# Splitting the last two heads' output product into two token halves, one for each column group of TensorE

## The chip, the cores and the metric

The kernel runs on one core of one Trainium2 chip. The metric is the device time of one execution in microseconds (us). Executions of the kernel before agree within 0.6%. For a comparison of ratios, runs of the kernel before and of the other kernel were taken in the same rounds on the same chip.

The engines are named as in the profile: PE is TensorE (matmuls), PEld its weight loads, DVE is VectorE, ACT is ScalarE, POOL is GpSimd.

## The reference

For 2048 tokens of width 640 the reference mixes two branches with a per-token gate. Branch A is linear attention with 32 heads of width 20 and softmax feature maps; branch B is a SwiGLU feed-forward network (FFN). What matters here is the end of branch A:

```python
phi_q = jnp.concatenate([_softmax(pq, axis=-1), _softmax(-pq, axis=-1)], axis=-1)
kv = jnp.einsum("bhsf,bhsd->bhfd", phi_k, v)
z  = jnp.einsum("bhsf->bhf", phi_k)
num = jnp.einsum("bhqf,bhfd->bhqd", phi_q, kv)      # the output product
den = jnp.einsum("bhqf,bhf->bhq", phi_q, z)[..., None] + 1e-6
o = num / den
# ... o @ wo is branch A; g * a + (1 - g) * b
```

## The kernel before

Tokens come in four query tiles (`bt`) of 512. For each, `oitem` computes the output product in three parts. Three heads have 3 x 40 = 120 features, so a group of three heads takes one 120-row matmul with 60 useful outputs (64 columns). Ten groups cover 30 heads; group 10 holds the last two heads, with 80 rows and 40 columns.

```python
def oitem(bt, part):
    buf = bt % 2
    pr = next_pair()                 # a pair of PSUM banks, least recently used of four
    pairs = []
    ms = [2 * part, 2 * part + 1]
    for i, m in enumerate(ms):
        for s in range(2):
            j = 2 * m + s
            if j >= NCH:             # NCH = 11
                continue
            if j == NCH - 1:         # the last two heads
                l, o = kvsb[0:80, j, 0:40], bank(2 * pr + i, 0, 512, 64, 104)
                r = phiT[0:80, buf, :, j, :]
            else:                    # output at partition 0 or 64: column group 0 or 64
                l, o = kvsb[0:120, j, :], bank(2 * pr + i, 0, 512, 64 * s, 64 * s + 64)
                r = phiT[0:120, buf, :, j, :]
            pairs.append((o, l, r, True, True, False))
    mm(pairs)
    if part < 2:
        copy("act", oT[:, buf, 2 * part:2 * part + 2, :], halves(pr, 512))
    else:
        copy("act", oT[:, buf, 4, :], bank(2 * pr, 0, 512))
        copy("act", hT[64:104, buf, 13, :], bank(2 * pr + 1, 0, 512, 64, 104))
```

The last two heads go into spare partitions of `hT`, the FFN's hidden tile, so that one contraction of the down-projection covers both. That projection (`ditem`, 128 tokens each) reads `hT` and `oT`, and issues all its matmuls in one call, so TensorE waits for all its operands before the first of them:

```python
def ditem(bt, u):
    ...
    ls = [(hT[:, buf, k, tok], wd[:, k, :]) for k in range(13)]
    ls += [(hT[0:104, buf, 13, tok], wd[0:104, 13, :])]
    ls += [(oT[:, buf, m, tok], wog[:, m, :]) for m in range(5)]
    ...
    mm([p for ab in zip(*half) for p in ab])
```

Waits come from a small tracker. For PSUM it works by whole banks, and a reader also waits for another engine's earlier readers of the same bank:

```python
if space == "psum":
    lo = lo // BANK * BANK
    hi = (hi + BANK - 1) // BANK * BANK
...
for k in rkeys:
    for kk in self._conflicts(k):
        req(self.lastw[kk], True)
        if k[0] == "psum":
            for s, v in self.readers[kk].items():
                req((s, v), False)
```

The order of issue is one long list, in which every engine takes its work in the order written. Around the first block (`C4` is the softmax normaliser of token tile 4 on VectorE, `O0.x` the three parts of the output product, `B5` and `A6` the next VectorE feature work, `D0.1` the first down-projection tile):

```
... Q6 F0.11 C4 O0.0 O0.2
c4 B5 A6 O0.1 C5 c5 Q7 Q8 B6 C6 c6 D0.1 B7 Q9 D0.3 ...
```

The softmax here doesn't subtract the row's maximum and nothing guards it: scores larger than these inputs give would overflow.

## Time and profile before

| | before |
|---|---|
| median of the first 3 runs (of 6) | 288.79 us (288.93 us) |
| span of the profiled run | 287.3 us |
| TensorE busy | 284.5 us (99%) |
| an output block, first matmul to the next stage | 1.42 us |
| first block to the first down-projection tile | 4.15 us |

The chain of work that ended last, in order of time, shows how complete the bound is. The columns are start, duration and what ran:

```profile
77.41 0.05 PE ps L308
77.46 207.92 PE ps L296 x1271
285.38 0.03 issue
285.41 0.32 DVE osb L733
```

From 77.46 us on there is a single piece of 208 us of TensorE work without a gap.

### The profile page before, as it was taken

The numbers are of one execution on the slowest core, as the hardware profiler recorded it, in microseconds if no ns is written. First come the engines' busy times: TensorE is split into PE (matmuls) and PEld (weight loads), VectorE is DVE, ScalarE is ACT, GpSimd is POOL, SyncE is SP. The second block draws the span as 40 slices with busy tenths as digits, with TensorE's granted clock in tenths as the row PEclk, the third lists the DMA queues.
The fourth block names the chain that finished last, engine by engine and source line by source line (L and its number), as shares of the span: only waits on it lengthen the run. The fifth ranks groups of instructions, "written<-read, shape, count | busy, mean of one in ns | idle before, by whom it ended". The sixth has DMA issues, their size and how long they took to land.

```text
span 287.3 us, 4960 instructions
## 1 busy us (share of the span) xinstructions
PE 284.5 (99%) x1975; PEld 174.7 (61%) x1975; DVE 163.4 (57%) x243; ACT 151.9 (53%) x252; POOL 159.9 (56%) x125
## 2 busy tenths in 40 slices
PE   8999999999999999999999999999999999999997
PEld 7667777675644545557775556675554446656776
DVE  2337748576569978589991565970317899000000
ACT  0767778576775566682535653225586552234112
POOL 8286999879446789836542438350754558501000
PEclk9999999999999999999999999999999999999999
DMA  7975797000010598202573002061020006210101
GB/s 236 200 117 120 114 292 257 3 1 2 2 47 0 130 283 162 50 2 50 68 155 73 3 1 50 2 155 37 2 50 0 3 1 123 52 46 0 49 23 48
DMA packets 48944, 21.62 MB, mean 75 GB/s; under 512 B 39384, under 2 KB 48792, under 8 KB 48920
## 3 DMA queue, kind: packets, MB, share of 16 engines
q1 hardware_dynamic: 47400, 20.43, 31.2%
q10 hardware_dynamic: 1520, 0.87, 1.0%
q8 instruction: 16, 0.26, 0.4%
q14 instruction: 8, 0.07, 0.1%
HBM read 9.29 MB, written 2.62 MB: 41 GB/s over the span
## 4 chain that ended last, share of the span: by engine, by line
PE 99%; DVE 0%; issue 0%
PE ps L296 97%; PE ps L478 1%; PE ps L308 1%; DVE osb L733 0%
## 5 line engine op out<-in xcount | busy, mean ns | idle before, releaser
L324 POOL TENSOR_TENSOR hT<-hT,us 128x512 bf16<-128x512 bf16 (+1 forms) x56 | 65.1, 1175 | 65.3 <-DVE hT L328 47.0
L328 DVE SCALAR_TENSOR_TENSOR hT<-hT,ps 128x512 bf16<-128x512 bf16 (+1 forms) x56 | 37.4, 682 | 67.0 <-ACT hT L314 53.3
L296 PE MATMUL ps<-xT,wg 128*128 128x512 bf16 x260 | 64.6, 379 | 0.0
L296 PE MATMUL ps<-xT,wu 128*128 128x512 bf16 x260 | 64.6, 379 | 0.0
L296 PE MATMUL ps<-wd,hT 128*128 128x320 bf16 (+2 forms) x462 | 63.9, 295 | 0.0
L324 POOL TENSOR_TENSOR ph<-eq,qc 128x1320 bf16<-128x1320 bf16 x16 | 42.4, 2648 | 25.6 <-DVE qc L638 20.8
L296 PEld LDWEIGHTS ps<-wd,hT 128*128 128x128 bf16 x462 | 44.5, 98 | 17.4
L296 PE MATMUL ps<-wqk,xT 128*128 128x320 bf16 x320 | 47.7, 299 | 0.0
L314 ACT ACTIVATE hT<-ps 128x512 bf16<-128x512 f32 (+2 forms) x60 | 35.7, 596 | 16.7 <-PE ps L296 16.5
L296 PEld LDWEIGHTS ps<-xT,wu 128*128 128x128 bf16 x260 | 25.4, 98 | 30.7
L314 ACT ACTIVATE us<-ps 128x512 bf16<-128x512 f32 (+1 forms) x56 | 33.5, 598 | 19.2 <-PE ps L296 18.2
L314 ACT ACTIVATE osb<-ps,omg 128x640 bf16<-128x640 f32 (+2 forms) x17 | 12.9, 758 | 55.7 <-PE ps L296 55.7
L296 PEld LDWEIGHTS ps<-xT,wg 128*128 128x128 bf16 x260 | 25.0, 98 | 27.8 <-ACT oT L314 0.8
L324 POOL TENSOR_TENSOR ekr<-ekr,krec 128x1280 bf16<-128x1280 bf16 x16 | 37.4, 2358 | 5.8 <-DVE krec L338 5.8
L296 PEld LDWEIGHTS ps<-wqk,xT 128*128 128x128 bf16 x320 | 30.5, 98 | 13.1 <-issue 0.4
L314 ACT ACTIVATE eq<-ps 128x640 bf16<-128x640 f32 x32 | 22.4, 704 | 20.8 <-POOL ph L324 10.7
L335 DVE TENSOR_REDUCE ksum<-ekr 128x64 f32<-128x1280 bf16 x16 | 23.5, 1470 | 11.7 <-ACT ekr L314 11.7
L314 ACT ACTIVATE ekr<-ps 128x640 bf16<-128x640 f32 x32 | 22.3, 704 | 8.7 <-PE ps L296 8.2
L335 DVE TENSOR_REDUCE qz<-eq 128x64 f32<-128x1280 bf16 x16 | 23.7, 1478 | 2.6 <-ACT eq L314 2.6
L296 PE MATMUL ps<-wog,oT 128*128 128x320 bf16 (+2 forms) x165 | 24.7, 294 | 0.0
L296 PE MATMUL ps<-wvg,xT 128*128 128x320 bf16 (+1 forms) x160 | 24.1, 299 | 0.0
L335 DVE TENSOR_REDUCE qw<-ez 128x64 f32<-128x1280 bf16 x16 | 23.6, 1476 | 0.0
(73 smaller groups left out, 189.4 us busy)
## 6 DMA issues: line engine op xcount, KB each, us to landing
out_dram<-osb SPq DMA_DIRECT2D x15, 160.0 KB, 1.9
wd<-in_B_w_down_dram SPq DMA_DIRECT2D x1, 2080.0 KB, 9.6
wg<-in_B_w_gate_dram SPq DMA_DIRECT2D x1, 1040.0 KB, 10.6
wu<-in_B_w_up_dram SPq DMA_DIRECT2D x1, 1040.0 KB, 12.8
wg<-in_B_w_gate_dram SPq DMA_DIRECT2D x1, 800.0 KB, 5.8
wu<-in_B_w_up_dram SPq DMA_DIRECT2D x1, 800.0 KB, 8.3
wog<-in_A_wo_dram SPq DMA_DIRECT2D x2, 375.0 KB, 7.1
xs<-in_A_x_dram ACTq DMA_DIRECT2D x3, 160.0 KB, 3.6
```

The source lines that it names most:

```text
L296: last = pe.matmul(o, lhsT=l, rhs=r, start=st, stop=sp_, skip_group_check=sk)
L308: last = pe.transpose(o, i, ident[0:k, 0:k])
L314: return run("act", lambda: act.activation(o, i, func, scale=scale), rd, [o])
L324: return run(e, lambda: eo.tensor_tensor(o, a, b, op), [a, b], [o])
L328: return run("dve", lambda: dve.scalar_tensor_tensor(out=o, in0=a, scalar=s, in1=b, op0=op0, op1=op1), rd, [o])
L335: return run("dve", lambda: dve.tensor_reduce(o, i, AX.X, ALU.add), [i], [o])
L478: last = pe.matmul(bank(2 * pr, 0, P), lhsT=c, rhs=c, start=True, stop=True)
```

## The change

An odd number of equal matmuls can't fill two column groups. The change cuts the odd one (the last two heads) into two halves of 256 tokens, one for each group. Since the halves then land in different partitions of the bank, it also cuts the copy out of PSUM in two, one on VectorE and one on ScalarE. The whole diff:

```diff
                 if j == NCH - 1:
-                    l, o = kvsb[0:80, j, 0:40], bank(2 * pr + i, 0, 512, 64, 104)
-                    r = phiT[0:80, buf, :, j, :]
+                    for g, p0 in enumerate((0, 64)):
+                        pairs.append((bank(2 * pr + i, 256 * g, 256 * g + 256, p0, p0 + 40),
+                                      kvsb[0:80, j, 0:40], phiT[0:80, buf, 2 * g:2 * g + 2, j, :],
+                                      True, True, False))
+                    continue
@@
             copy("act", oT[:, buf, 4, :], bank(2 * pr, 0, 512))
-            copy("act", hT[64:104, buf, 13, :], bank(2 * pr + 1, 0, 512, 64, 104))
+            copy("dve", hT[64:104, buf, 13, 0:256], bank(2 * pr + 1, 0, 256, 0, 40))
+            copy("act", hT[64:104, buf, 13, 256:512], bank(2 * pr + 1, 256, 512, 64, 104))
```

## The prediction

> **What bounds the kernel now.** I read the page first (busy shares, then the chain that ended last), then the timeline of each of the four places where the changed code runs, then the groups by form for durations.
>
> ```profile
> PE 284.5 (99%) x1975; PEld 174.7 (61%) x1975; DVE 163.4 (57%) x243; ACT 151.9 (53%) x252; POOL 159.9 (56%) x125
> PE 99%; DVE 0%; issue 0%
> ```
>
> The first line is the busy time of each engine, the second the shares of the chain that ended last. The whole span is one unbroken run of TensorE (PE) work. From 77 us to the end no matmul starts later than its pace allows, apart from the edges of the four output-product blocks below. So TensorE time taken out shortens the run one for one, and any new stall of TensorE lengthens it one for one.
>
> The changed product runs in four short blocks, one per query tile (called O0 to O3 here), of eleven matmuls each. The timeline of TensorE at two FFN groups and at O0:
>
> ```profile
> 220.72 1.24 PE L296 MATMUL ps<-xT,wg 128*128 128x512 bf16 x5
> 221.80 1.24 PE L296 MATMUL ps<-xT,wu 128*128 128x512 bf16 x5
> ...
> 126.00 1.49 PE L296 MATMUL ps<-phiT,kvsb 120*64 120x512 bf16 x11
> 127.11 0.38 PE L296 MATMUL ps<-phiT,kvsb 120*64 120x512 bf16 x1
> 127.42 0.31 PE L296 MATMUL ps<-wqk,xT 128*128 128x320 bf16 x1
> ```
>
> Five 512-wide matmuls of full width advance the clock by 221.80 - 220.72 = 1.08 us, 0.216 each. Eleven in O0 take 126.00 to 127.42 = 1.42 us, not 2.38: they run two at a time in the two column groups (outputs at partitions 0 and 64). Single records confirm it: starts come in pairs 3 to 11 ns apart, the pairs 0.216 apart. Group 0 has five of the eleven, group 64 has six, because the odd one (the last two heads, 80*40) also writes at partition 64. The last matmul, at 127.11, therefore runs alone: half the array idles for one 0.216 us slot in each block. That is what the change is after.
>
> Who empties the banks, at O0 (the timeline of ScalarE and VectorE, and TensorE's next stage):
>
> ```profile
> 127.42 2.75 PE L296 MATMUL ps<-wqk,xT 128*128 128x320 bf16 x19
> 128.20 0.59 ACT L314 ACTIVATE hT<-ps 40x512 bf16<-40x512 f32 x1
> 128.81 1.02 ACT L314 ACTIVATE oT<-ps 128x1024 bf16<-128x1024 f32 x1
> 129.15 0.28 DVE L638 SCALAR_TENSOR_TENSOR qc<-qz,g,qd 128x64 f32<-128x64 f32 x1
> 129.35 0.82 DVE L324 TENSOR_TENSOR ez<-eq,zb 128x1280 bf16<-128x1280 bf16 x1
> 130.15 2.74 PE L296 MATMUL ps<-wd,hT 128*128 128x320 bf16 x19
> ```
>
> The `wd,hT` row at 130.15 is the first down-projection tile after O0. Its code waits for every operand before its first matmul, and the last of them is the `oT` copy that ScalarE ends at 128.813 + 1.024 = 129.84. The margin is 0.31 us. Meanwhile VectorE is busy without a break with the normalisers of the softmax features until the `qc` row ends at 129.435.
>
> **What the Trainium skill says.** TensorEngine Tiling (Array Packing), section Key Properties: tiles work independently, and a change of tiling mode drains TensorE. The trace agrees with both: the pairs start within 11 ns, and a change of mode costs 0.096 us at each edge of a block (0.31 against 0.216). The same page, PSUM Bottleneck, says that tiling does not speed the emptying of PSUM and advises to use both ScalarE and VectorE; the change does that, and the trace shows where it will pinch. PSUM — Partial Sum Buffer, on bank collisions, says that two engines must not touch one bank in one 32-partition quadrant at once, while different quadrants are allowed. The new copies read partitions 0-39 and 64-103, different quadrants, but the kernel's bookkeeping guards by whole bank, reads against reads of another engine included. So the ScalarE copy must wait for the VectorE copy. VectorE: DVE Perf Modes, section Two Vector instructions with no wait between them: an instruction whose output starts in another quadrant than the last one's starts only when the earlier ones have finished. The new copy writes at partition 64 behind `qc` at partition 0, so I give it no overlap; no row of the kernel before shows this case.
>
> **The change part by part.**
>
> TensorE. One 80*40 matmul over 512 tokens becomes two of 256, one in each column group. Each group then has five full slots and a half: 5.5 x 0.216 instead of 6 x 0.216, so 0.108 us less per block, 0.43 us for four. The added weight load (99 ns for 40 columns in the trace) goes ahead beside other work, as the 109 ns loads of this block do now; it barely fits beside a 107 ns stream, so 0.108 is the most.
>
> ScalarE. The 40x512 copy (592 ns) becomes 40x256. From the 512- and 1024-wide rows (590 and 1022 ns) the slope is 0.84 ns per element, so about 592 - 256 x 0.84 = 377 ns. It saves 0.21 us on an engine that is not the bound.
>
> VectorE. A new copy of 40x256 from PSUM, f32 to bf16. The rows of that kind are 120x160 in 314 ns and 128x640 in 824 ns (the groups by form), 1.06 ns per element between them: 314 + 96 x 1.06 = 416 ns. Four of them are 1.7 us, and where they stand matters.
>
> The new wait, block by block. In program order the VectorE copy comes after all VectorE work issued before the block, and ScalarE stands still until it is done.
>
> At O0 the normaliser of tile 4 (1.48 us reduction and six small steps, ending with `qc` at 129.435) is issued just before the block. So: copy starts 129.435 + 0.035 (the usual gap between dependent VectorE steps) = 129.47 and ends 129.89; ScalarE follows 0.035 later (seen from VectorE to ScalarE), 129.92, + 0.377 = 130.30; the remaining `oT` copy starts 0.024 later and ends 130.32 + 1.024 = 131.35; TensorE follows about 0.07 later (median of ScalarE to weight load), 131.42. Before it was 130.146: **+1.27 us**, already net, since the 0.108 gained in this block only makes TensorE arrive earlier at the same wait.
>
> At O1, O2 and O3 VectorE has long been idle:
>
> ```profile
> 158.11 0.69 DVE L328 SCALAR_TENSOR_TENSOR hT<-hT,ps 128x512 bf16<-128x512 bf16 x1 [6.48 <-ACT hT L314]
> 201.96 0.68 DVE L328 SCALAR_TENSOR_TENSOR hT<-hT,ps 64x512 bf16<-64x512 bf16 x1 [9.51 <-ACT us L314]
> 260.23 0.69 DVE L328 SCALAR_TENSOR_TENSOR hT<-hT,ps 128x512 bf16<-128x512 bf16 x1 [14.48 <-ACT hT L314]
> ```
>
> Brackets give the idle time of VectorE before each row. Those gaps span the blocks at 153.6, 196.9 and 255.7. In O2 the matmul ends near 197.4, the copy near 197.85, and ScalarE, which first has an output scaling and an `oT` copy to do, comes to its half only at 198.28: no wait. O1 and O3 have the same order. But VectorE work that now runs ahead of the block must wait behind the copy: at O1 a 1.48 us reduction (to about 156.1, next VectorE row 158.1), at O2 a normaliser of 2.9 us (to about 200.8, next row 201.96). Both fit. So each gives its 0.108 us: **-0.32 us**.
>
> Sum: 1.27 - 0.32 = +0.95 us on 288.79, **289.7 us**.
>
> **The rivals.**
>
> Clean gain: no stall at O0, -0.43, 288.36 us. For it speaks that TensorE is the whole chain and that the other three blocks have room; against it the 0.31 us margin and the 1.75 us (128.17 to 129.92) for which ScalarE would have to stand. It would need the copy to find VectorE free. One in ten.
>
> Halves that don't run side by side, or whose weight loads show: 0 in place of -0.32, giving 290.1 us. For it speaks that 99 ns of loading hardly hides behind 107 ns; against it, that the groups already run separate queues and that loads of both groups overlap now. Two in ten, in part.
>
> Later knock-on: VectorE is dense until 151.6 and everything in it moves 0.45 us later; a feature tile or a PSUM pair could come late to TensorE. Against it: of the next stages the tightest pair is freed near 139.4, and TensorE wants it at 141.8 before the shift of 1.27. It would add some tenths, 290.0 to 290.4 us. One in ten.
>
> **Range and chances.** The centre is 289.7. The size of the stall is a sum of four read-off durations, each good to some tens of ns; the gains are at most 0.32. The three runs of before spread from 288.74 to 289.39, which is the larger part of the doubt. I take 288.9 to 290.2 for 8 in 10; the clean gain lies outside it. Two per cent would be 5.8 us, far beyond anything found: faster 0.005, same 0.985, slower 0.01.
>
> **What would show it.** Right: at O0 a VectorE copy of 40x256 into `hT` starting near 129.47, ScalarE's 40x256 copy behind it with an idle bracket of about 1.7 us put down to VectorE, the next `oT` copy near 130.3, and the down-projection tile starting near 131.4 after an idle stretch of TensorE of 1.2 to 1.4 us. In O1 to O3 the block shrinks from 1.42 to about 1.32 us, with no idle bracket on ScalarE's half copy. Wrong: the copy found in front of the normaliser, a TensorE gap elsewhere, or blocks that stay 1.42 us long.

## The result and the profile after

The changed kernel takes 290.09 us (289.69 to 290.15, 6 runs) against 288.93 us (288.72 to 289.39, 6 runs): the ratio is 1.0034, with a 95% interval of 1.0021 to 1.0047. A ratio is the mean time of one kernel's runs over that of the other's of the same rounds, so it is not quite the ratio of the medians quoted. By the 2% at which this study calls a kernel faster or slower it is "same"; but the interval lies wholly above 1, so it is a loss of about 1 us, clear of the noise.

The page of the changed kernel, busy shares and the chain's shares by engine:

```profile
PE 284.3 (99%) x1979; PEld 174.6 (61%) x1979; DVE 166.2 (58%) x247; ACT 151.0 (52%) x252; POOL 159.4 (55%) x125
PE 99%; issue 0%; DVE 0%
```

TensorE has four matmuls more and is busy 0.2 us less, yet the span went from 287.3 to 288.4 us. The busy shares hide the reason. The chain of the changed kernel in order of time shows it:

```profile
77.67 52.74 PE ps L296 x272
130.40 1.24 issue
131.65 154.91 PE ps L296 x1003
```

The one piece of 208 us is now two, with 1.24 us between them in which TensorE did nothing ("issue" means that the profile saw no single wait to name). What stands there is in the timeline of the changed kernel, TensorE first and then VectorE, ScalarE and GpSimd; a bracket gives the idle time before a row and what ended it:

```profile
126.20 1.39 PE L296 MATMUL ps<-phiT,kvsb 120*64 120x512 bf16 x12
127.51 2.89 PE L296 MATMUL ps<-wqk,xT 128*128 128x320 bf16 x20
131.65 3.97 PE L296 MATMUL ps<-wd,hT 128*128 128x320 bf16 x28 [1.24 <-issue]
...
129.35 0.28 DVE L638 SCALAR_TENSOR_TENSOR qc<-qz,g,qd 128x64 f32<-128x64 f32 x1
129.67 0.42 DVE L320 CAST hT<-ps 40x256 bf16<-40x256 f32 x1
130.12 2.70 DVE L324 TENSOR_TENSOR ez<-eq,zb 128x1280 bf16<-128x1280 bf16 x1
...
130.12 0.38 ACT L314 ACTIVATE hT<-ps 40x256 bf16<-40x256 f32 x1 [1.75 <-DVE hT L320]
130.52 1.02 ACT L314 ACTIVATE oT<-ps 128x1024 bf16<-128x1024 f32 x1
...
129.72 2.42 POOL L324 TENSOR_TENSOR ph<-eq,qc 128x1320 bf16<-128x1320 bf16 x1 [1.52 <-DVE qc L638]
```

Follow the chain backwards. The down-projection tile at 131.65 follows ScalarE's `oT` copy, which ends at 131.55. That copy stands behind ScalarE's half copy, which waited 1.75 us for VectorE's half copy. And that one stands behind the normaliser, whose last step is the `qc` row. The matmuls themselves did what was intended: the block takes from 126.20 to 127.51, 1.32 us in place of 1.42.

In the second block (same timeline, VectorE and ScalarE) the same copies cost nothing, because VectorE was idle and waited for TensorE, and ScalarE got to its half later and shows no bracket:

```profile
155.67 0.42 DVE L320 CAST hT<-ps 40x256 bf16<-40x256 f32 x1 [2.79 <-PE ps L296]
156.53 0.38 ACT L314 ACTIVATE hT<-ps 40x256 bf16<-40x256 f32 x1
```

**A sharper measure than the time.** The start-up varies from run to run: in the traces used here the first block's first matmul starts anywhere from 125.80 to 126.76 us. From that matmul on the traces repeat closely: the time from the first down-projection tile to the end differs by at most 0.012 us between kernels that have the same later blocks. So I compare two stretches in each trace: from the first block's first matmul to the first down-projection tile (called the *lead*), and from that tile to the end of the span (the *rest*). Start times are from the single records.

| kernel | lead, us | rest, us | lead + rest against before |
|---|---|---|---|
| before | 4.150 | 157.121 | |
| changed | 5.450 | 156.799 | +0.98 |

The lead lost 1.30 us and the rest gained 0.32 us.

### The profile page after: what moved, and what is told of

Its sections match the earlier page's. It is cut to its first block, busy times and chain, and to the rows that moved or that the text cites. A ratio compares the mean times of both kernels' runs of the same rounds, so it can differ in the third digit from the quotient of the medians.

```text
span 288.4 us, 4971 instructions
## 1 busy us (share of the span) xinstructions
PE 284.3 (99%) x1979; PEld 174.6 (61%) x1979; DVE 166.2 (58%) x247; ACT 151.0 (52%) x252; POOL 159.4 (55%) x125
## 4 chain that ended last, share of the span: by engine, by line
PE 99%; issue 0%; DVE 0%
PE ps L296 97%; PE ps L478 1%; PE ps L308 1%; DVE osb L737 0%
## 5 line engine op out<-in xcount | busy, mean ns | idle before, releaser
L324 POOL TENSOR_TENSOR ph<-eq,qc 128x1320 bf16<-128x1320 bf16 x16 | 41.8, 2615 | 28.5 <-DVE qc L638 23.8
L314 ACT ACTIVATE hT<-ps 128x512 bf16<-128x512 f32 (+2 forms) x60 | 34.9, 582 | 18.4 <-PE ps L296 16.4
```

The lines of the kernel that those rows point to most:

```text
L314: return run("act", lambda: act.activation(o, i, func, scale=scale), rd, [o])
L324: return run(e, lambda: eo.tensor_tensor(o, a, b, op), [a, b], [o])
```

## The experiments

The theory: all the loss is ScalarE waiting for the VectorE copy in the first block, because the copy stands behind the normaliser in VectorE's order; the split matmuls gain 0.108 us in each block. Rival A: the halves or their weight loads cost TensorE time. Rival B: the late VectorE work after the first block holds TensorE; it has something to it at first sight, as the feature product `ez` behind the copy took 2.70 us in place of 0.82. Eight kernels ran, all with right results, with five rounds each.

### Both copies on ScalarE

```diff
-            copy("dve", hT[64:104, buf, 13, 0:256], bank(2 * pr + 1, 0, 256, 0, 40))
+            copy("act", hT[64:104, buf, 13, 0:256], bank(2 * pr + 1, 0, 256, 0, 40))
```

> Matmul halves kept, both copies of the halves on ScalarE. My theory (all of the loss is ScalarE standing behind the VectorE copy at O0; the halves themselves gain 0.108 us per block): two copies of 0.38 take the place of one of 0.59, so the next oT copy ends 0.19 later than in the kernel before, and the first down-projection tile starts about 4.10 us after O0's first matmul (before 4.15, after 5.45); from O0's first matmul to the end about 0.37 us less than before, 288.5 us. Rival A (the halves or their added weight load cost TensorE time): at best as slow as before. Rival B (the VectorE stretch after O0 runs late and holds TensorE): also about as before or better, since nothing was added to VectorE; B does not separate here.

Measured: lead 4.127, rest 156.798, together -0.35 us. The timed median was 288.62 us against 289.03 (ratio 0.9988, interval 0.9971 to 1.0004, so not proven by the times alone). ScalarE's timeline shows its three copies one after the other, with no wait:

```profile
128.96 0.78 ACT L314 ACTIVATE hT<-ps 40x256 bf16<-40x256 f32 x2
129.76 1.02 ACT L314 ACTIVATE oT<-ps 128x1024 bf16<-128x1024 f32 x1
```

The lead is 0.03 us longer than expected and otherwise as the theory has it. Rival A falls: with the same halves and the same loads, the kernel is not slower.

### The copies alone

```diff
-            copy("act", hT[64:104, buf, 13, :], bank(2 * pr + 1, 0, 512, 64, 104))
+            copy("dve", hT[64:104, buf, 13, 0:256], bank(2 * pr + 1, 0, 256, 64, 104))
+            copy("act", hT[64:104, buf, 13, 256:512], bank(2 * pr + 1, 256, 512, 64, 104))
```

This is against the kernel before; the matmul stays whole.

> The matmul left whole, only the copy split (VectorE first half, ScalarE second half). My theory: the stall at O0 as in the changed kernel and no gain elsewhere: the down-projection tile 5.4 us after O0's first matmul, +1.25 us to the end, 290.2 us. Rival A (the halves cost): as fast as before, 288.9.

Measured: lead 5.467, rest 157.109, together +1.31 us; 290.08 us (ratio 1.0039, interval 1.0026 to 1.0052). The loss comes with the copies and without the halves. The timeline of ScalarE in this kernel has the same wait:

```profile
130.70 0.38 ACT L314 ACTIVATE hT<-ps 40x256 bf16<-40x256 f32 x1 [1.76 <-DVE hT L320]
```

### The two copies swapped

```diff
-            copy("dve", hT[64:104, buf, 13, 0:256], bank(2 * pr + 1, 0, 256, 0, 40))
             copy("act", hT[64:104, buf, 13, 256:512], bank(2 * pr + 1, 256, 512, 64, 104))
+            copy("dve", hT[64:104, buf, 13, 0:256], bank(2 * pr + 1, 0, 256, 0, 40))
```

> The whole change, with its two copy lines swapped: ScalarE copies its half first, VectorE second. The VectorE copy keeps its place behind the normaliser and stays just as late. My theory: ScalarE no longer waits for VectorE; the oT copy ends near its old time, the VectorE copy ends about 0.1 us before TensorE needs it; no stall, 0.108 gained in all four blocks, 0.43 us less than before: 288.5 us, 4.04 us from O0's first matmul to the down-projection tile. Rival B (the late VectorE stretch is what costs; the feature product after the copy took 2.70 us in place of 0.82): the copy still pushes that product behind GpSimd's, so the loss of some 1 us stays, 289.9 us.

Measured: lead 4.253, rest 156.797, together -0.22 us; 288.33 us against 289.03 (ratio 0.9981, interval 0.9969 to 0.9993). Its ScalarE and VectorE timelines:

```profile
128.19 0.38 ACT L314 ACTIVATE hT<-ps 40x256 bf16<-40x256 f32 x1
128.59 1.02 ACT L314 ACTIVATE oT<-ps 128x1024 bf16<-128x1024 f32 x1
...
129.46 0.42 DVE L320 CAST hT<-ps 40x256 bf16<-40x256 f32 x1
129.91 2.70 DVE L324 TENSOR_TENSOR ez<-eq,zb 128x1280 bf16<-128x1280 bf16 x1
```

Swapping two lines takes the stall away, although VectorE does the same work in the same order: the copy is as late as before and `ez` still takes 2.70 us. So rival B falls. The gain is 0.21 us short of the expectation, all of it in the lead. The VectorE copy ends at 129.88 and the down-projection tile starts at 130.24, not at the 130.03 that the expected lead of 4.04 us gives. The records of TensorE's own sequencer show why (they stand in the packed trace; no view prints them): three wait instructions start there at 129.918, 130.029 and 130.135, one after the other. The first is the wait for VectorE. The two after it had nothing left to wait for, since what they wait for had last been signalled at 129.63 or before, and still they cost 0.11 us each.

### The first block issued before the normaliser

```diff
-... Q6 F0.11 C4 O0.0 O0.2
+... Q6 F0.11 O0.0 O0.2 C4
 c4 B5 A6 O0.1 ...
```

> The whole change, with the two block parts of O0 issued before the normaliser of tile 4 instead of behind it, so that the VectorE copy stands before the normaliser. My theory: copy starts as soon as TensorE is done with the halves (some 1.0 us after O0's first matmul), no wait on ScalarE, 4.04 us to the down-projection tile, 0.43 us less than before: 288.5 us. The normaliser comes 0.8 us later, and the feature product behind it should again start before GpSimd and take 0.82 us. Rival A: no better than before. If normaliser lateness matters, TensorE stalls later on.

Measured: lead 4.044, rest 156.792, together -0.43 us; 288.43 us against 289.03 (ratio 0.9982, interval 0.9970 to 0.9994). This is the full gain of the halves. The copy now waits for TensorE, not the other way round, and the normaliser follows it:

```profile
127.26 0.42 DVE L320 CAST hT<-ps 40x256 bf16<-40x256 f32 x1 [0.39 <-PE ps L296]
127.70 1.49 DVE L335 TENSOR_REDUCE qw<-ez 128x64 f32<-128x1280 bf16 x1
...
130.56 0.82 DVE L324 TENSOR_TENSOR ez<-eq,zb 128x1280 bf16<-128x1280 bf16 x1
...
128.47 0.38 ACT L314 ACTIVATE hT<-ps 40x256 bf16<-40x256 f32 x1
```

`ez` is back at 0.82 us, and the later normaliser disturbs nothing. This kernel beats both the kernel before and the changed one, in the times as in the traces.

### The change in the first block alone, and in the last three alone

```diff
-                if j == NCH - 1:
+                if j == NCH - 1 and bt == 0:       # the other run: bt > 0
                     for g, p0 in enumerate((0, 64)):
...                                                 # else as before, in matmuls and copies
```

> The change in the first query tile's block alone, the other three as before. My theory: +1.3 us, 290.2 us; the down-projection tile 5.45 us after O0's first matmul; the other blocks 1.42 us long. If the loss were spread over the four blocks: about +0.25.

> The change in the last three blocks, the first as before. My theory: 0.32 us less than before, 288.6 us; 4.15 us from O0's first matmul to the down-projection tile, the other three blocks 1.32 us long, no new stall. If the loss were spread over the four blocks: about +0.75.

Measured for the first block alone: lead 5.454, rest 157.117, together +1.30 us; 289.92 us against 289.00 (ratio 1.0038, interval 1.0017 to 1.0060). For the last three alone: lead 4.150, rest 156.792, together -0.33 us; 288.46 us against 289.00 (ratio 0.9984, interval 0.9961 to 1.0007, so not proven by the times). The two add up to +0.97 us; the whole change has +0.98. The loss sits in the first block and nowhere else, and each of the others gives 0.33 / 3 = 0.11 us.

### The part with the last two heads last of the three

```diff
-... C4 O0.0 O0.2
-c4 B5 A6 O0.1 C5 ...
+... C4 O0.0 O0.1
+c4 B5 A6 O0.2 C5 ...
```

> The whole change, with O0's part that holds the last two heads issued after the other two parts. ScalarE then waits for VectorE with nothing behind it but its own half. My theory: the half copy still ends about 4.3 us after O0's first matmul because VectorE is as late as before, and the down-projection tile reads it: it starts about 4.37 after O0's first matmul, 0.22 later than before; with the gain of the other blocks -0.1 us in all, 288.8 us. If only the number of waits mattered and not what stands behind them, it would be as slow as the changed kernel.

Measured: lead 6.390, rest 156.793, together +1.91 us; 292.22 us against 289.00 (ratio 1.0098). I had missed that this edit also puts the copy behind `B5` and `A6`, the next feature product and reduction of VectorE, so the expectation didn't fit the kernel. The timelines of VectorE, ScalarE and TensorE:

```profile
131.80 0.42 DVE L320 CAST hT<-ps 40x256 bf16<-40x256 f32 x1
132.26 0.38 ACT L314 ACTIVATE hT<-ps 40x256 bf16<-40x256 f32 x1 [2.97 <-DVE hT L320]
132.59 0.70 PE L296 MATMUL ps<-wd,hT 128*128 128x320 bf16 x4 [2.19 <-DVE hT L320]
```

The copy moved from 3.47 us after the block's start (129.668 - 126.197 in the changed kernel) to 5.61 (131.803 - 126.195), and the lead grew from 5.45 to 6.39. It is a stronger form of the same fault: what counts is the copy's place in VectorE's order. Here the tile waits for VectorE's copy itself. Four of the six timed runs had a lower TensorE clock (told in the last section); the two at full clock, 290.71 and 290.92 us, are 1.7 and 1.9 us above the kernel before, in accord with the trace.

The next run does what that one was meant to do:

```diff
-... C4 O0.0 O0.2
-c4 B5 A6 O0.1 C5 ...
+... C4 O0.0 O0.1
+O0.2 c4 B5 A6 C5 ...
```

> The run before this moved the part with the last two heads too far: it also came behind the next feature product and reduction of VectorE, so the copy stood 2.1 us later in VectorE's order. Here that part comes last of O0's three, but still right behind the normaliser, so the VectorE copy is where the changed kernel has it. My theory: the copy runs about 3.47 to 3.89 us after O0's first matmul as in the changed kernel, ScalarE's half ends at about 4.30, and the down-projection tile starts at about 4.4 (4.37 plus up to 0.1 of TensorE's own waits), against 5.45 in the changed kernel; to the end about 161.2 us, 288.9 us timed. If what stands behind ScalarE's wait made no difference: 5.45.

Measured: lead 4.256, rest 156.792, together -0.22 us; 288.76 us against 288.93 (ratio 0.9991, interval 0.9978 to 1.0005, so not proven by the times alone). The wait of ScalarE is still there:

```profile
129.72 0.38 ACT L314 ACTIVATE hT<-ps 40x256 bf16<-40x256 f32 x1 [0.83 <-DVE hT L320]
```

Nothing that TensorE soon needs stands behind it any more, and 1.19 of the 1.30 us that the lead had lost are back. The lead is 0.14 us shorter than I expected, and for a reason that I had wrong: the first down-projection tile takes tokens 128 to 255, which lie in VectorE's half, so it does not read ScalarE's half at all. Indeed it starts at 130.055, before ScalarE's half copy ends at 130.103. It waits for VectorE's copy, which ends at 129.692; from there to the tile it is 0.363 us, as in the run with swapped copies (129.879 to 130.242, also 0.363).

### Not tried

The tracker could guard PSUM by quadrants of partitions in place of whole banks, which should take away ScalarE's wait with the copies left in their order. That was not built, so that it does, and what it gives, is not shown. Nor was a kernel tried that puts the two halves into different banks.

## Why the prediction was right

The time predicted was 289.7 us, in a range of 288.9 to 290.2; measured were 290.09 us. The forecast difference of +0.95 us measured +0.98 in the traces; the medians differ by 1.16. The time lies 0.4 us above the centre and only 0.11 below the range's upper end, so that it lay inside the range owes something to chance. What is known of the 0.4 us is not the mechanism: 0.14 is the kernel before, whose median was 288.79 in the first three runs and 288.93 in all six, and in the two profiled runs 0.20 is start-up, before the first block (126.197 against 125.996).

**TensorE's halves.** Expected was 0.108 us in each block. The blocks went from 1.423 to 1.316 us, and the last three blocks alone gave 0.33 us. The doubt about the weight loads came to nothing: the matmuls behind the halves start 0.113 us after them, against 0.108 for the stream alone (half of 0.216), and the block still ends 0.107 us earlier.

**The new wait in the first block.** The steps, each counted from the block's first matmul:

| step | predicted | measured |
|---|---|---|
| VectorE copy starts | 3.47 | 3.471 |
| its duration | 0.416 | 0.418 |
| ScalarE's half starts | 3.92 | 3.923 |
| its duration | 0.377 | 0.379 |
| last `oT` copy ends | 5.35 | 5.351 |
| down-projection tile starts | 5.42 | 5.450 |

Predicted values are the prediction's clock times less 125.996. Only the last step was off, by 0.03 us: TensorE followed 0.099 us behind ScalarE, not 0.07. The durations, interpolated from rows of other widths, held to 2 ns. The copy started 0.031 us after the `qc` row's end and `ez` 0.031 us after the copy, where before `ez` had started 0.083 us ahead of `qc`'s end. That agrees with what the prediction had quoted from the Trainium skill's VectorE: DVE Perf Modes, Two Vector instructions with no wait between them.

**No wait in the other three blocks.** This was right: no bracket on ScalarE's half there, and the rest of the run is 0.32 us shorter, three times 0.107.

**The rivals.** The clean gain failed in the first block only, and the kernel with the block issued earlier shows that it was to be had: -0.43 us. The margin of 0.31 us that the prediction set against it was not all slack, since some 0.10 us of it is TensorE's step behind ScalarE. With both copies on ScalarE the `oT` copy ended 0.185 us later than before (4.026 us after the block's start against 3.841), and the tile was already 0.08 us late (4.127 against 4.044 in the kernel with the block issued earlier). Halves that do not run side by side are ruled out by their records, which start 3 to 4 ns apart. The knock-on was underestimated in size and still harmless. I had VectorE 0.45 us later; in fact the reduction behind `ez` starts at 132.74, 2.45 us later than before when counted from the block's start (6.546 against 4.092). I had not seen that `ez` would now start behind GpSimd's product and be held by it. In all ten traces it takes 2.69 to 2.71 us where it starts after that product, and 0.82 where it starts before. The Trainium skill's SBUF — State Buffer, SBUF: two separate sides, says of a VectorE instruction with two SBUF inputs and a GpSimd instruction that reads SBUF that whichever starts first has the shared ports for its whole length, while the other is blocked fully. The trace agrees roughly: `ez` ends at 132.82, 0.68 us after the product's end at 132.14, a little less than its own 0.82. The rest of the run does not show any of this to 0.01 us.

**Small slips in the prediction, without effect on its sum.** The cost at an edge of a block, 0.31 less 0.216, is 0.094 us and not 0.096. Behind the reduction the normaliser has five small steps and not six.

## What to carry to other kernels

When work is moved to an engine that is "only 57% busy", what counts is where its instruction lands in that engine's order, and what else waits for it there; look at that stretch of the timeline, not at the share. If two engines empty one bank under a guard by bank, let the one that is on time go first, or issue the pair where the other one is free. And where most of a span repeats to 0.01 us from trace to trace, compare stretches between two fixed events: here this settled effects of 0.1 us that the times could not.

## What the Trainium skill lacked or had wrong

- **Perfetto Trace Analysis**, Identifying Dependency Chains, says that extra wait instructions may stand ahead of an instruction that waits for several engines, but not what they cost. Here TensorE started 0.363 us after the end of the work it waited for when that wait stood first in the list (in three runs), and 0.099 us after it in the changed kernel, where the wait for ScalarE stands in the list's last wait instruction; the satisfied waits in between are 0.11 us apart.
- **TensorEngine Tiling (Array Packing)**, Key Properties, names the drain at a change of mode without a figure. At each edge of a block the next matmul started 0.093 to 0.095 us later than the stream alone has it, in both kernels (0.310 us against 0.216 at 512 columns, 0.229 against 0.136 at 320): some 0.75 us in all for the eight edges.
- **TensorE: Matmul & The Clock Gate**, Part 3, says that matmuls start strictly in program order. In the kernel before, the 80*40 matmul is the third of the second block in program order, and its record starts 4 ns after that of the fourth (153.860 and 153.856), which goes to the other column group; the other three blocks show the same, 3 to 4 ns. The difference is small beside what the records resolve, so it is a hint rather than proof.
- The same page, Why this matters for your kernels, warns of gaps over about 3 us. In the run with the part moved too far, TensorE idled 2.19 us in the trace. Four of its six runs had a mean granted clock of 0.994 and took 291.93 to 292.79 us; the two at full clock took 290.71 and 290.92. All runs of the other kernels had the full clock. An estimate from these numbers: 0.006 of 291 us is 1.7 us, as much as these four runs are longer than the two (292.48 against 290.82 in the mean). Where in them the clock fell, and whether the idle time was the cause, no trace shows, since the profiled one was at full clock.
